# The sixth batch's routing in a fused block attention and top-1 expert kernel: begun a pair sooner, its small operations on GpSimd

## The chip, the cores and the metric

One core of one Trainium2 chip. The metric is device time of one execution in microseconds (us), the lower the better. Engines are named as the profile names them: PE is TensorE (PEld its weight loads), DVE is VectorE, ACT is ScalarE, POOL is GpSimd, SP is SyncE, which here only issues DMAs. The clock of TensorE has two levels, 1.2 and 2.4 GHz; the profile gives the granted share of the higher one.

## The reference

```python
# q, k, v: (8, 8, 576, 64)
mask = (pos[:, None] // 64) >= (pos[None, :] // 64)
attn = softmax(where(mask, q @ k.T / 8, -1e9))
x = (attn @ v) as 4608 tokens x 512
logits = x @ w_gate                     # 512 x 8
e_idx = argmax(logits, axis=1)
gate_w = softmax(logits)[row, e_idx]
eom = 1 / (1 + exp(-(x @ w_output_gate)))
for e in range(8):
    mask = e_idx == e
    out[mask] = gate_w[mask] * eom[mask, e] * (relu(x[mask] @ w1[e]) @ w2[e])
```

Block-causal attention over 8 batches of 8 heads; each of the 4608 tokens then goes to the one expert with its largest logit, and its result is scaled by two gates.

## The kernel before

**Attention.** Heads go in pairs, four pairs a batch, 32 pairs in all; one turn of the loop at L1208 attends one pair (`attend`, L1169). A turn interleaves three pairs: the scores and exponentials of pair p (`softmax`, L332), the transposes of pair p-1's probabilities (`flip`, L436) and the product with the values of pair p-2 (`values`, L472). The order on TensorE is written out by hand as a string in `attend`, of which each letter is one step: S scores, F a flip group, V values, t one tick.

```python
for x in "S.Ft.SVFSV.FttSFt.":
```

So a turn has four ticks, and every generator in the list `later` makes one step at each of them. Flip groups turn probabilities in the one PSUM tile `ps_f`, which ACT and DVE each copy half of into `pT` (L446); the next group waits until both have done so. The maxima of the scores (`nmx`, L375) are DVE's, the exponentials (L368, L419) ACT's. Q and K of a coming pair are split into two 16-bit parts by POOL (`split_qk`, L141, tiles `natq`, `natk`, `sp`) and turned by a DMA transpose that SP issues (`turn_qk`, L160, `qk<-sp`); there are three `qk` tiles, so the transpose of pair p+3 waits for the last scores of pair p (L413).

**Routing.** When a batch's values are done, a generator `finish_batch` (L504) is put into `later`. It makes the logits (L532), turns them (L571, L581), multiplies them by the reciprocal of the softmax sums, reduces over heads into `L` (L587), takes the maximum `mx`, and then runs a chain of small operations on tiles of 40 or 5 columns (`on_pool`, L595): `d`, `eq`, `er`, `oh` (the one-hot choice), `z`, then a prefix sum over tokens on TensorE (L672 to L678), the slot `sli`, and the gate by `se`, `zs` and a reciprocal into `idg` (L718). Five indirect DMAs on POOL, the scatters (L724), write token and gate into a table in DRAM, `tab_d`. `rows` (L508) turns the attention result by TensorE, scales it on DVE (`xn`, L516) and `store` (L524) sends it to `x_d` by SP.

The flag `slow` marks batches 0 to 4: their small operations go to POOL and are spread over ticks by `part`. Batches 5 to 7 keep them on DVE in one tick. For b == B - 3, the sixth batch (b = 5), the row blocks are moved out by a second generator, `spread_rows`. With a batch's values ending in the turn after its last pair but one, the sixth batch's route runs while pairs 26 to 29 are attended.

**Experts.** From pair 30 on, `route_first` (L761) picks the first expert from the counts of batches 0 to 5, `fetch_ids` (L908) reads the table after the scatters, `fetch_x` (L924) gathers tokens into `xg` and weights are loaded. The pool `ld`, which holds `natq`, `natk` and `sp`, is given back at L1215, and two of the `xg` tiles, which are cleared by POOL at L1222, lie in its place. Then steps of 256, 128 or 64 tokens pass through the experts (L1062, L1103) until the end, TensorE being busy almost throughout.

The order of a queue is not wholly the program's: within the marks `issue_after` and `behind`, a scheduler places instructions on ACT, DVE, POOL and SP. A queue is in order: what stands behind a waiting instruction waits too.

## Time and profile before

| | us |
|---|---|
| median of 3 runs | 738.97 |
| the three runs | 737.44, 738.97, 741.25 |
| the profiled execution | 742.68 |
| its span, first to last instruction | 741.1 |
| PE busy | 701.0 (95%) |
| DVE busy | 543.8 (73%) |
| ACT busy | 499.1 (67%) |
| POOL busy | 317.5 (43%) |

The profile tells one execution; its rows have the start in us from the span's start, the duration, the engine, the line, what is written and read, and in square brackets how long the engine stood idle before and what ended that ("issue" means that the profile shows no wait). An engine's share over the whole span says little here, as attention, hand-over and experts have different limits, so stretches are looked at one by one. The attention stage lies in about the first 325 us.

### The profile page before, as it was taken

Reading aid. Unit: us, or ns where it says so; the run is one execution under the profiler, and the core shown is the slowest. Engines: PE = TensorE matmul, PEld = TensorE weight load, DVE = VectorE, ACT = ScalarE, POOL = GpSimd, SP = SyncE. Lnnn points to the kernel's source line nnn. Section 1 sums busy time; section 2 is a strip of 40 time slices with the busy share of each in tenths; the row PEclk is TensorE's granted clock in tenths of the full one; section 3 lists DMA queues with packets and bytes.
Section 4 is the critical chain, followed back from the end, with each engine's and each line's share of the span. In section 5 each row is a group of like instructions: output and inputs, shape, how many; then the busy total and the mean of one; then the engine's idle time right before and its main releaser. Section 6 shows DMA issues by size and latency. Waiting matters only on the chain. (4 is left out here: it accounts for less than half of the span.)

```text
span 741.1 us, 21145 instructions
## 1 busy us (share of the span) xinstructions
PE 701.0 (95%) x8277; PEld 497.3 (67%) x8298; DVE 543.8 (73%) x948; ACT 499.1 (67%) x1097; POOL 317.5 (43%) x407
## 2 busy tenths in 40 slices
PE   5999999998999996989999999999999999999994
PEld 4677777766777764757568666876577676767761
DVE  4877988887888886887777658955588577858830
ACT  4888888886888875774356558765577487758630
POOL 4375468776686873015365523321223133311011
PEclk9999999999999998899999999999999999999998
DMA  7989898999999984458546796977999999775601
GB/s 199 215 189 208 142 206 146 168 195 187 201 211 184 177 129 74 131 171 233 138 143 130 215 283 191 296 91 241 259 302 363 247 335 321 273 224 195 237 31 46
DMA packets 235997, 146.85 MB, mean 198 GB/s; under 512 B 187120, under 2 KB 203568, under 8 KB 235888
## 3 DMA queue, kind: packets, MB, share of 16 engines
q1 hardware_dynamic: 227136, 125.85, 71.0%
q0 software_dynamic: 8208, 19.29, 9.1%
q8 instruction: 67, 1.10, 0.7%
q14 instruction: 42, 0.34, 0.2%
q10 hardware_dynamic: 544, 0.26, 0.1%
HBM read 126.43 MB, written 19.34 MB: 197 GB/s over the span
## 5 line engine op out<-in xcount | busy, mean ns | idle before, releaser
L1083 PEld LDWEIGHTS <-w1b 128*128 128x128 f16 (+1 forms) x2208 | 176.2, 98 | 25.9 <-issue 4.5
L1083 PE MATMUL ps_s<-xt,w1b 128*128 128x256 f16 (+5 forms) x1920 | 175.5, 253 | 0.7 <-DVE w1b L961 0.4
L1118 PE MATMUL ps_t<-w2b,hh 128*128 128x512 f16 (+1 forms) x539 | 162.1, 379 | 0.0
L961 DVE TENSOR_TENSOR w2b<-w2f,w2b 128x1024 bf16<-128x1024 f32 x80 | 92.9, 1222 | 83.3 <-ACT w2b L959 81.1
L375 DVE TENSOR_REDUCE nmx<-ps_s 128x1 f32<-128x512 f32 (+4 forms) x224 | 130.5, 617 | 24.4 <-PE ps_s L364 9.7
L368 ACT ACTIVATE pt<-ps_s,nmx 128x256 f32<-128x256 f32 (+3 forms) x256 | 132.6, 534 | 11.5 <-DVE nmx L375 6.8
L1126 POOL DMA_INDIRECT out_dram<-ys,ids x38 | 48.1, 1266 | 171.3 <-ACT ys L1125 93.6
L1118 PE MATMUL ps_t<-w2b,hl 128*128 128x512 f16 x280 | 106.1, 379 | 1.1
L961 DVE TENSOR_TENSOR w1b<-w1f,w1b 128x1024 bf16<-128x1024 f32 x80 | 93.5, 1220 | 8.9 <-ACT w1b L959 8.7
L1118 PEld LDWEIGHTS <-hh 128*128 128x128 f16 x560 | 54.4, 98 | 61.6
L1125 ACT ACTIVATE ys<-ps_t,ids 128x512 f32<-128x512 f32 (+1 forms) x38 | 25.9, 685 | 98.1 <-PE ps_t L1118 77.2
L959 ACT CAST w1b<-w1f 128x1024 f16<-128x1024 f32 x80 | 78.8, 1045 | 13.5 <-DMA w1f<-in_moe_w_dram 11.6
L482 PE MATMUL ps_t<-pT,vv 128*64 128x256 f32 (+3 forms) x512 | 83.7, 448 | 1.1 <-DVE sums L549 0.8
L446 DVE COPY pT<-ps_f 128x512 f32<-128x512 f32 x93 | 63.7, 685 | 25.2 <-PE ps_f L443 20.8
L356 PE MATMUL ps_s<-qk 64*128 64x256 f16 (+1 forms) x1152 | 72.2, 256 | 7.7 <-DMA qk<-sp 3.4
L959 ACT CAST w2b<-w2f 128x1024 f16<-128x1024 f32 x80 | 78.0, 1044 | 1.5 <-DMA w2f<-in_moe_w_dram 1.3
L928 POOL DMA_INDIRECT xg<-x_d,ids x38 | 54.3, 1428 | 31.5 <-issue 10.4
L356 PEld LDWEIGHTS <-qk 64*128 64x128 f16 x1152 | 47.3, 96 | 21.5 <-issue 13.8
L446 ACT COPY pT<-ps_f 128x512 f32<-128x512 f32 x93 | 54.6, 587 | 9.1 <-PE ps_f L443 5.3
L1091 ACT ACTIVATE hh<-ps_s 128x1024 f16<-128x1024 f32 (+2 forms) x46 | 38.9, 846 | 30.4 <-PE ps_s L1083 27.9
L443 PEld LDWEIGHTS ps_f<-ident,pt 64*128 64x128 f32 x1116 | 42.1, 138 | 25.3 <-ACT pt L368 11.4
L724 POOL DMA_INDIRECT tab_d<-idg,sli x40 | 41.9, 1048 | 38.3 <-DVE sli L692 30.5
(221 smaller groups left out, 1055.3 us busy)
## 6 DMA issues: line engine op xcount, KB each, us to landing
w1f<-in_moe_w_dram SPq DMA_DIRECT2D x80, 512.0 KB
w2f<-in_moe_w_dram SPq DMA_DIRECT2D x80, 512.0 KB
vv<-in_v_dram SPq DMA_DIRECT2D x64, 128.0 KB
x_d<-xn SPq DMA_DIRECT2D x32, 256.0 KB
natk<-in_k_dram SPq DMA_DIRECT2D x14, 512.0 KB
natq<-in_q_dram SPq DMA_DIRECT2D x28, 256.0 KB
hh<-in_moe_w_dram SPq DMA_DIRECT2D x4, 512.0 KB
hl<-in_moe_w_dram SPq DMA_DIRECT2D x4, 512.0 KB
```

The source lines that it names most:

```text
L356: nc.tensor.matmul(ps[:, ab, c:c + m], qk[rows, cq, P * t:P * t + P], cols(qk[rows, ck], x, kind), start=(i == 0), stop=(i == 2 and c + m ...
L368: last_exp[0] = nc.scalar.activation(probs[t][:, ab], ps[:, ab, c0:c0 + n], AF.Exp, bias=nmx[:, t, ab:ab + 1], accum_out=sums[:, t, 2 * hp ...
L375: last_max[0] = nc.vector.tensor_reduce(o, x, AX.X, ALU.max, negate=True)
L443: nc.tensor.transpose(ps[:, h, 64 * i:64 * i + 64], src[rows], ident[rows, rows])
L446: copy(to[:, h], ps[:, h].rearrange("p (s c) -> p s c", c=P))
L482: nc.tensor.matmul(pa[o, P * j:S0].rearrange("p (t h n) -> p t h n", h=2, n=64), vv[:, j, a0 + ab], pT[:, :, x:x + P * m].rearrange("p h ( ...
L928: nc.gpsimd.indirect_dma_start(out=xg[i % NXG][:, h], out_offset=None, in_=x_d[0:nx, :], in_offset=IOA(ap=ids[i][:, h, 0:1].bitcast(U32), ...
L959: nc.scalar.copy(hi, src)
L961: eng.tensor_tensor(lo, src, hi, ALU.subtract)
L1083: nc.tensor.matmul(ph[:, f4].rearrange("p (h n) -> p h n", n=w), wv[:, cc, f, :], xv[:, cc, :, 0:w], start=(k == 0), stop=(k == 3 * KD - 1))
L1118: nc.tensor.matmul(py, hv[:, f, h], wv[:, f, :], start=(k == 0), stop=(k == 3 * KF - 1))
L1126: nc.gpsimd.indirect_dma_start(out=out, out_offset=IOA(ap=ids[i][0:r, h, 0:1].bitcast(U32), axis=0), in_=ys[0:r], in_offset=None, bounds_c ...
```

## The change

It puts the sixth batch (flag `mid`) nearly onto the path of the batches ahead of it. Its wide logits come in the same tick as its narrow ones, and two ticks fall out, so that the maximum `mx` is taken in pair 26 in place of pair 27. `d`, `eq`, `oh`, the memset, `z`, `se` and `zs` go to POOL behind its last instruction; `er` and the choice come a few ticks later; `exp` of `d` comes earlier on ACT. `spread_rows` is gone, the row blocks are written out between the steps (last block in pair 27, blocks 0 and 1 in pair 28, 2 and 3 in pair 29). The scatters stand at the four ticks of pair 29.

```diff
@@ -539,7 +539,7 @@
         def keep(c0, c1, pm):
             nc.scalar.copy(lgT[:, c0:c1], pm[:, 0:c1 - c0])
 
-        held, rush = [], b == B - 1
+        held, rush, mid = [], b == B - 1, b == B - 3
         pm = ps_t.tile([P, 512], F32, name="ps_t")
         nc.tensor.matmul(pm[0:64, P:P + NP], ident[:, 64:128], sumL, start=True, stop=True)
         if not rush:
@@ -557,7 +557,8 @@
             yield
         else:
             keep(S0, S, pm)
-            yield
+            if not mid:
+                yield
             nc.scalar.activation(rec, sums, AF.Copy, bias=1e-9)
             pm = ps_t.tile([P, 512], F32, name="ps_t")
             logits(0, S0, pm)
@@ -565,7 +566,8 @@
             yield
             nc.vector.reciprocal(rec, rec)
             yield
-            yield
+            if not mid:
+                yield
         pm = ps_t.tile([P, 512], F32, name="ps_t")
         for t in range(LAST):
             nc.tensor.transpose(pm[:, P * t:P * t + P], lgT[:, Q0[t]:Q0[t] + P], ident)
@@ -590,36 +592,28 @@
         nc.vector.tensor_reduce(mx, lg, AX.X, ALU.max)
         mxb = mx.unsqueeze(2).broadcast_to([P, NT, E])
         slow = b < B - 3
-        eng = nc.gpsimd if slow else nc.vector
+        pool = slow or mid
+        eng = nc.gpsimd if pool else nc.vector
 
         def on_pool(*ops):
 
             for op, args in ops:
-                with behind() if slow else nullcontext():
+                with behind() if pool else nullcontext():
                     ins = getattr(eng, op)(*args)
-                if slow:
+                if pool:
                     last_pool[0] = ins
 
         def after(last):
-            return tc.issue_after(last[0].ins) if slow else nullcontext()
+            return tc.issue_after(last[0].ins) if pool else nullcontext()
 
         def part(n):
 
             for x in range(n if slow else 0):
                 yield
 
-        def part_rows(t):
-
-            if slow:
-                rows(t)
-                yield
-                store()
-
-        def spread_rows():
-
-            for n, t in ((2, LAST), (0, 0), (2, 1), (0, 2), (0, 3)):
-                for x in range(n):
-                    yield
+        def part_rows(t, always=False):
+
+            if slow or always:
                 rows(t)
                 yield
                 store()
@@ -630,16 +624,22 @@
         oh = small.tile([P, NT, E], F16, name="oh")
         z = small.tile([P, NT, E], F32, name="z")
         yield from part(3)
+        if mid:
+            yield
         on_pool(
             ("tensor_tensor", (d, lg, mxb, ALU.subtract)),
             ("tensor_scalar", (eq, d, 0.0, None, ALU.is_equal)),
             ("tensor_tensor", (eq, eq, erev.unsqueeze(1).broadcast_to([P, NT, E]), ALU.mult)),
         )
-        yield from part_rows(LAST)
+        if mid:
+            yield
+        yield from part_rows(LAST, mid)
         yield from part_rows(0)
         with after(last_max):
             nc.vector.tensor_reduce(er, eq, AX.X, ALU.max)
         yield from part(1)
+        if mid:
+            yield
         erb = er.unsqueeze(2).broadcast_to([P, NT, E])
         on_pool(
             ("tensor_tensor", (eq, erb, erev.unsqueeze(1).broadcast_to([P, NT, E]), ALU.subtract)),
@@ -647,18 +647,17 @@
             ("memset", (oh[64:128, LAST, :], 0.0)),
             ("tensor_tensor", (z, lz, oh, ALU.mult)),
         )
-        if slow:
+        if pool:
             with after(last_exp):
                 nc.scalar.activation(d, d, AF.Exp)
         yield from part(1)
         yield from part_rows(1)
         yield from part_rows(2)
         yield from part(1)
-        if b == B - 3:
-            later.append(spread_rows())
-            yield
-            yield
-            yield
+        if mid:
+            yield
+            yield from part_rows(0, True)
+            yield from part_rows(1, True)
             yield
         elif not slow:
             yield
@@ -690,7 +689,8 @@
         sli = small.tile([P, NT], I32, name="sli")
         if not slow:
             last_hot[0] = nc.vector.tensor_copy(sli, sl)
-            nc.scalar.activation(d, d, AF.Exp)
+            if not mid:
+                nc.scalar.activation(d, d, AF.Exp)
         se = small.tile([P, NT], F32, name="se")
         with after(last_max):
             nc.vector.tensor_reduce(se, d, AX.X, ALU.add)
@@ -699,6 +699,8 @@
             nc.vector.tensor_reduce(zs, z, AX.X, ALU.add)
         yield from part(1)
         yield from part_rows(3)
+        if mid:
+            yield
         with after(last_exp):
             last_gate[0] = nc.scalar.activation(zs, zs, AF.Exp, scale=-1.0)
         yield from part(1)
@@ -717,8 +719,14 @@
         with after(last_max):
             nc.vector.reciprocal(idg.bitcast(F32)[:, b, :, 1], zs)
         yield from part(2)
+        if mid:
+            rows(2)
         for t in range(NT):
             r = ROWS[t]
+            if mid and t in (1, 2):
+                store()
+            if mid and t == 1:
+                rows(3)
 
             with behind():
                 last_pool[0] = nc.gpsimd.indirect_dma_start(
@@ -733,8 +741,9 @@
             tc.add_to_no_dep_group("scatters", sc)
             scatters.append(sc)
             if b < B - 1 and t < LAST:
-                yield
-                if b < B - 3 or b == B - 3 and t == 0:
+                if not mid or t < 3:
+                    yield
+                if slow:
                     yield
         if rush:
             for t in range(NT):
```

Three places show what moved. On POOL, from the end of the split of pair 31 on, before (`se` and `zs` are the gate's tiles, `xg` the token tiles, `row` what `route_first` makes):

```order
L155 TENSOR_TENSOR sp<-natk_104,sp 128x2x4x64
L724 DMA tab_d<-idg,sli 37120x2 x6
L1222 MEMSET xg_6324 128x1024
L1222 MEMSET xg_6326 128x1024
L916 TENSOR_LOAD row_202
```

and now:

```order
L155 TENSOR_TENSOR sp<-natk_104,sp 128x2x4x64 [waits Pool_49]
L732 DMA tab_d<-idg,sli 37120x2 [waits DMASW5_49]
L602 TENSOR_SCALAR se<-se 128x5 [waits DVE_49]
L1231 MEMSET xg_6324 128x1024 [waits DMAHW3_49,DMAHW4_49,DMAHW0_49,Pool_49]
L1231 MEMSET xg_6326 128x1024
L602 TENSOR_SCALAR zs<-zs 128x5 [waits Activation_49]
L602 TENSOR_TENSOR zs<-zs,se 128x5 [waits Pool_49]
L732 DMA tab_d<-idg,sli 37120x2 [waits DMASW6_49,DVE_49]
L732 DMA tab_d<-idg,sli 37120x2 [waits DMASW7_49]
```

`se` and `zs` are new on this queue, and the two memsets, which wait for three DMA queues, stand ahead of `zs` and of the five scatters.

On DVE, pair 28, between its second maxima and its second copy of `pT`, before:

```order
L599 TENSOR_TENSOR eq<-er,erev 128x40 [waits DVE_49]
L696 TENSOR_REDUCE se<-d 128x5 [waits Activation_49]
L599 TENSOR_SCALAR oh<-eq 128x40 [waits DVE_49]
L599 TENSOR_SCALAR se<-se 128x5 [waits DVE_49]
L599 MEMSET oh 64x4 [waits DVE_49]
L599 TENSOR_TENSOR z<-L,oh 128x40 [waits DVE_49]
L683 TENSOR_REDUCE add<-oh 128x8
L699 TENSOR_REDUCE zs<-z 128x5 [waits DVE_49]
L685 TENSOR_TENSOR run_cnt<-run_cnt,add 128x8 [waits DVE_49]
L599 TENSOR_SCALAR zs<-zs 128x5 [waits Activation_49]
L599 TENSOR_TENSOR zs<-zs,se 128x5 [waits DVE_49]
L446 COPY pT<-ps_f 128x4x128 [waits PE_49]
```

and the same place now:

```order
L375 TENSOR_REDUCE nmx<-ps_s 128x1 [waits PE_49]
L375 TENSOR_REDUCE nmx<-ps_s 128x1
L446 COPY pT<-ps_f 128x4x128 [waits PE_49]
L394 TENSOR_REDUCE qlast_108<-qk 64x2x64 [waits DMAHW4_49]
L394 TENSOR_REDUCE qlast_108<-qk 64x2x64
L375 TENSOR_REDUCE nmx<-ps_s 128x1 [waits PE_49]
```

The chain between the maxima and the copy is gone. In pair 29 DVE now has, from the first copy of `pT` on:

```order
L446 COPY pT<-ps_f 128x4x128 [waits PE_49]
L516 TENSOR_TENSOR xn<-ps_t,rec 128x512 [waits DMAHW5_49,PE_49]
L375 TENSOR_REDUCE nmx<-ps_s 128x1 [waits PE_49]
L375 TENSOR_REDUCE nmx<-ps_s 128x1
L720 RECIPROCAL idg<-zs 128x5 [waits Pool_49]
L446 COPY pT<-ps_f 128x4x128 [waits PE_49]
L394 TENSOR_REDUCE qlast_109<-qk 64x2x64 [waits DMAHW3_49]
L394 TENSOR_REDUCE qlast_109<-qk 64x2x64
```

Here the sixth batch's reciprocal, which waits for POOL, stands between the second maxima (128x1) and the second copy of `pT`.

On PE, pair 26, behind its first flip group, before:

```order
L513 MATMUL ps_t<-ident,xT 128x128 [waits Activation_49]
L513 MATMUL ps_t<-ident,xT 128x128 x3
L544 MATMUL ps_t<-sumL,ident 64x4 [waits DVE_49]
L534 MATMUL ps_t<-xT,wg_bd 32x64 x4
L356 LDWEIGHTS qk
L356 MATMUL ps_s<-qk 128x256 [waits Activation_49]
```

and now:

```order
L513 MATMUL ps_t<-ident,xT 128x128 [waits Activation_49]
L513 MATMUL ps_t<-ident,xT 128x128 x3
L544 MATMUL ps_t<-sumL,ident 64x4 [waits DVE_49]
L534 MATMUL ps_t<-xT,wg_bd 32x64 x4
L534 MATMUL ps_t<-xT,wg_bd 32x512 [waits DVE_49]
L534 MATMUL ps_t<-xT,wg_bd 32x512 x3
L356 LDWEIGHTS qk
L356 MATMUL ps_s<-qk 128x256 [waits Activation_49]
```

The wide logits (32x512) stand ahead of the next scores and wait for DVE.

## Rows read from the trace of the kernel before

**Rows 1.** Stretches of pairs 25 to 29: us, busy us by engine, PEclk, DMA share, GB/s

```profile
243.30:252.20 8.90, 8.90 (x149) 6.74 (x147) 7.73 (x16) 7.49 (x24) 8.12 (x14) 1.00 1.20 203
252.20:262.70 10.50, 10.34 (x170) 7.02 (x168) 8.06 (x23) 8.39 (x27) 5.48 (x12) 1.00 0.68 166
262.70:271.60 8.90, 8.90 (x152) 6.52 (x152) 7.55 (x17) 7.29 (x23) 8.29 (x12) 1.00 0.82 128
271.60:286.00 14.40, 10.54 (x153) 7.72 (x148) 12.81 (x35) 8.29 (x27) 6.25 (x7) 0.91 0.53 62
286.00:301.40 15.40, 13.10 (x153) 9.60 (x152) 9.21 (x18) 7.59 (x23) 6.64 (x7) 0.75 0.46 75
```

**Rows 2.** Order of time on PE, pairs 28 and 29

```profile
281.51 0.46 PE L443 MATMUL ps_f<-ident,pt 64*128 64x64 f32 x8 [2.69 <-DVE pT L446]
...
283.41 1.11 PE L513 MATMUL ps_t<-ident,xT 128*128 128x128 f32 x4 [0.92 <-DVE xT L499]
284.32 1.65 PE L413 MATMUL ps_s<-qk,qlast 128*128 128x256 f16 x9
...
293.11 0.41 PE L356 MATMUL ps_s<-qk 64*128 64x256 f16 x4 [0.96 <-issue]
294.54 0.58 PE L356 MATMUL ps_s<-qk 64*128 64x256 f16 x3 [1.02 <-issue]
```

**Rows 3.** Order of time on PE, pairs 26 and 27

```profile
261.71 0.92 PE L413 MATMUL ps_s<-qk,qlast 128*128 128x256 f16 x9
...
269.57 0.46 PE L443 MATMUL ps_f<-ident,pt 64*128 64x64 f32 x8
```

**Rows 4.** Order of time on DVE, pair 28

```profile
275.54 1.83 DVE L599 TENSOR_SCALAR eq<-d 128x40 f32<-128x40 f32 x1
...
280.60 0.17 DVE L599 TENSOR_TENSOR zs<-zs,se 128x5 f32<-128x5 f32 x1
280.68 0.68 DVE L446 COPY pT<-ps_f 128x512 f32<-128x512 f32 x1
```

**Rows 5.** Instructions of L599: ns shortest/median/longest, first and last start, form

```profile
L599 POOL TENSOR_SCALAR eq<-d x5: 331/332/332, 84.6 to 237.7; 128x40 f32<-128x40 f32 x5
...
L599 POOL TENSOR_SCALAR zs<-zs x5: 231/232/234, 109.2 to 262.2; 128x5 f32<-128x5 f32 x5
...
L599 DVE TENSOR_SCALAR eq<-d x3: 185/195/1828, 275.5 to 345.8; 128x40 f32<-128x40 f32 x3
```

**Rows 6.** Order of time on POOL, pairs 24 to 30

```profile
237.36 0.25 POOL L599 TENSOR_TENSOR d<-L,mx 128x40 f32<-128x40 f32 x1 [3.50 <-DVE mx L590]
...
276.17 1.16 POOL L155 TENSOR_TENSOR sp<-natk,sp 128x512 f16<-128x512 f32 x1
...
287.35 0.99 POOL L724 DMA_INDIRECT tab_d<-idg,sli  x1 [8.95 <-DVE sli L692]
...
293.79 1.84 POOL L1222 MEMSET xg<- 128x1024 f32 x2 [0.42 <-issue]
308.42 0.78 POOL L917 DMA_DIRECT2D ids<-tab_d  x1 [12.78 <-DVE qlast L394]
```

**Rows 7.** Order of time on DVE, pairs 26 and 27

```profile
254.97 0.68 DVE L516 TENSOR_TENSOR xn<-ps_t,rec 128x512 f32<-128x512 f32 x1
...
267.62 0.69 DVE L446 COPY pT<-ps_f 128x512 f32<-128x512 f32 x1 [0.70 <-PE ps_f L443]
```

**Rows 8.** Order of time on PE, pair 26, the narrow logits

```profile
254.60 0.32 PE L534 MATMUL ps_t<-xT,wg_bd 128*32 128x64 f32 x8
```

**Rows 9.** Order of time on SP, two transposes of Q and K

```profile
167.16 6.07 SPq L164 DMA_TRANSPOSE qk<-sp  x1
...
286.04 2.72 SPq L164 DMA_TRANSPOSE qk<-sp  x1
```

**Rows 10.** Order of time on PE, scores that waited for the first of these

```profile
177.98 0.34 PE L356 MATMUL ps_s<-qk 64*128 64x128 f16 x6 [1.60 <-DMA qk<-sp]
```

**Rows 11.** DMA share in tenths, 284 to 294 us in 40 equal slices

```profile
DMA  0000000000000899998069999799899992501321
```

## The prediction

> **What bounds the kernel now.** I number pairs 0 to 31 and write p28 for pair 28; the sixth batch is b = 5, its values end in p25, its route runs in p26 to p29. I first cut the attention stage into pairs, from one last row maximum (L375 of 576 columns) to the next [rows 1]. p25 to p27 take 8.90, 10.50 and 8.90 us, 9.43 on average, with TensorE busy in all but 0.16 us: here TensorE sets the pace, and GpSimd's and DVE's small work is free while it hides beside it. Then p28 takes 14.40 and p29 15.40, 5.0 and 6.0 us over that average, at granted clocks of 0.91 and 0.75. These two pairs are the only place where the change can win much.
>
> Next I asked why TensorE stands there, in its order of time [rows 2]. In p28 it stops for 2.69 us until 281.51, released by DVE's copy of pT (the copy frees the PSUM tile ps_f for the next flip group), then for 0.92 us until 283.41; right after it nine L413 matmuls take 1.65 us where p26's took 0.92 [rows 3], with the granted clock down between its two levels, 1.2 and 2.4 GHz (0.91 over the pair). In p29 it stops for 0.96 and 1.02 us inside one group of score matmuls, released by "issue": no wait that the profile shows.
>
> Then DVE's order [rows 4]: the copy that TensorE waited for started at 280.68, late because the route's chain stands ahead of it on the same engine, among it one eq of 1.83 us. The same instruction takes 0.185 us when nothing disturbs it [rows 5]. It ran while GpSimd's subtraction of 276.17 to 277.33 ran [rows 6]. In p26 the end of L413 was at 262.63 (261.71 + 0.92) [rows 3], and the like copy started at 267.62 [rows 7], 4.99 after it. This is the measure used below: T is the end of a pair's L413, and the next pair's second copy of pT starts at T + 5.0 when nothing is late. The third flip group, which needs it, starts at 269.57 [rows 3], T + 6.9; so the copy has a slack of 6.9 - 5.0 - 0.69 = 1.2 us.
>
> **The change part by part.**
> *The chain leaves DVE.* d, eq twice, the second eq, oh, se, the memset, z and the zs pair go to GpSimd, ten instructions, and exp of d no longer stands between two pairs of exponentials on ScalarE. GpSimd pays 0.23 to 0.33 us for such an operation [rows 5], beside DVE's and TensorE's work. With the chain gone, p28 has nothing that other pairs lack: -5.0.
>
> Here a page and the rows can be weighed. The eq of 1.83 us overlaps GpSimd's subtraction, as said. The Trainium skill, "SBUF — State Buffer", section "Who interferes with whom", says that VectorE and GpSimd share one port pair under an exclusive lock that is held for a whole instruction. By that rule 1.64 of eq is a wait that ends when eq itself stands in GpSimd's queue, and the -5.0 stands; were it a cost of that place in DVE's order, another instruction would inherit it and the sum would be 1.64 higher. No row separates the two.
>
> *A pair sooner.* The 512 column logits now stand right behind the 64 column ones in p26, and take the ps_t buffer whose xn DVE finishes at 255.65 (254.97 + 0.68) [rows 7]; TensorE is ready for them at 254.92 (254.60 + 0.32) [rows 8]. +0.7. The transposes of lgT and the reduction L move from p27 and p28 to p26; the 1.24 us of L now delay p27's first maxima instead of p28's. Unhidden they are +1.24, fully hidden 0; with DVE busy in 7.55 of p27's 8.90 us [rows 1] I take +0.4. Together +1.1.
>
> *GpSimd's queue.* d waits for mx: in the fourth batch such a wait took 3.50 us [rows 6]. The split of p31 ended at 277.33 before [rows 6]; waits, three operations and two scatters ahead of it make it some 4 us later, about 281. It is needed when the transpose of p31 may start, which is the end of p28's L413 (284.32 + 1.65 = 285.97 [rows 2], SP issues at 286.04 [rows 9]); in the changed kernel that end comes at about 281.7. It just fits: 0. The er reduction comes three steps after its inputs: 0.
>
> *The stores.* The 64 row store goes ahead of vlast and one 256 KB store ahead of p31's transpose on SP. Each is ready some 5 us earlier, and one store less runs beside the transpose: 0.
>
> *The new wait.* This is the term that decides. GpSimd's order is now: se, two memsets of xg, the two zs operations, the scatters. The memsets wait for the transposes of p29, p30 and p31, because xg lies where their sources lay. And DVE's reciprocal of zs stands right ahead of p29's second copy of pT and waits for the zs operations. Before, the memsets stood behind the scatters and nobody waited for them [rows 6]. So p29's copy now waits for the landing of p31's transpose. Let L be the time from its issue, at about T + 0.1, to its landing. Behind it come two memsets (1.84 us [rows 6]), twice some 0.23 for zs [rows 5], and some 0.5 for the reciprocal and the handovers, an estimate from the 0.17 of a like small operation on DVE [rows 4]: the copy starts at about T + L + 2.8, and the third flip group at T + L + 3.5. The stall is L + 3.5 - 6.9 = L - 3.4. Bounds of L: at least the 2.72 us that SP takes to issue it [rows 9]; at most 10.8, as the one issued at 167.16 [rows 9] released TensorE at 177.98 [rows 10]. For p31's own, the DMA share stays high until about 292.5 [rows 11] (slices of 0.25 us from 284), 6.5 us after its issue. I take 6.5, the same transfer: +3.1. At the ends it is 0 and +7.4.
>
> *The scatters.* They now start behind the reciprocal, at some T + 9, five that took 6.0 us from 287.35 to the idle 0.42 us ahead of the memset [rows 6], and end near T + 15. The first read of the table is issued at 308.42, after 12.78 us of idle [rows 6]; that cover shrinks to some 3 us. I price it at 0; if the landing needs more than those 3 us, the first gathers are late.
>
> *The gaps of p29.* Its 6.0 us are gaps without a visible wait and the half clock behind them. They begin while GpSimd issues five scatters in a row from 287.35 on [rows 6], and p29 had just come out of a slow stretch; both conditions leave that place. Bounds: all stay, 0; all go, -6.0.
>
> **The sum** against the profiled execution (742.68, span 741.1 and 1.6 around it): -5.0 + 1.1 + 3.1 = -0.8. With the gaps kept 741.9, with the gaps gone 735.9. The median of the runs, 738.97, lies 3.7 below the profiled one, so the typical run seems to hold only part of those gaps: from it, -0.8 gives 738.2. I expect between 735.9 and 738.2, nearer the lower end: **736.6**.
>
> **The rivals.**
> *The new wait costs nothing, the gaps go* (faster). If L is below 3.4 the stall vanishes; for it speaks that fewer transfers run beside p31's transpose, against it the 6.5 us of the same transfer. Time: 742.68 - 5.0 + 1.1 - 6.0 = 732.8.
> *The transpose lands late* (slower). With L = 10.8 the stall is 7.4, and TensorE may fall to half clock behind it as at 283.41, which I price at the 0.73 us by which those L413 grew [rows 2, 3] and about as much again for the rest, 1.4. From the median: 738.97 - 5.0 + 1.1 + 7.4 + 1.4 = 743.9. It is slower than before from L = 7.3 on (L - 3.4 over 3.9). For it: p31's transpose and the wait are now in one chain with no slack. Against it: the 10.8 was in a stretch with V, Q and K loads in the queues.
> *It moves nothing*: p28's loss merely walks to p29 with its clock: 738.97.
> *GpSimd is too slow for the chain.* Its eq takes 0.332 where DVE's shortest is 0.185 [rows 5]; ten such add 1 to 1.5 us. If it is late with eq in p27, er holds DVE's queue: +1.5, 740.5 from the median. [...]
>
> **How the numbers follow.** Forecast (735.3 to 739): 0.50. Free wait with gaps gone: 0.27. Late landing: 0.12. Nothing: 0.07. Slow GpSimd: 0.04. About 0.5%, 3.7 us, is what a measurement here can tell from no change; that is under 735.3 and over 742.7. The forecast gives 0.06 of its own to faster, the free wait all of its 0.27; the late landing gives 0.10 to slower, the rest is in between: 0.33, 0.57, 0.10. The range reaches from just under the free-wait case to a stall with L near 9: **732.0 to 741.5**.
>
> **What would show it.** p28 near 9.5 us, with no stall on DVE's pT copy and eq on GpSimd at 0.33; p26 with a wait of some 0.7 us ahead of the logits. In p29 GpSimd's first memset released by the DMA of qk, DVE idle before the reciprocal until GpSimd's zs, TensorE idle some 3 us ahead of its third flip group. I am wrong if the reciprocal does not wait, if p28 stays above 12 us, or if TensorE's stall in p29 is over 5 us.

## The result, and the profile after

The changed kernel took 743.47 us in the median of 21 runs (738.4 to 750.47), the kernel before 738.76 in 21 runs beside them: ratio 1.0078, 95% interval 1.0054 to 1.0102. Slower by 0.8%, and 2.0 us above the range's upper end. A ratio, here and below, leaves out executions more than 1.5% above the fastest of their kernel, so it can differ from the quotient of the medians beside it. The change's profiled execution took 744.06, span 742.1.

First the same cut into pairs as in [rows 1], here for p26 to p30 of the changed kernel (us, busy us by engine, PEclk, DMA share, GB/s; the last line sums them):

```profile
258.64:270.22 11.58, 10.79 (x174) 7.45 (x172) 8.82 (x24) 8.61 (x27) 1.26 (x4) 1.00 0.77 198
270.22:279.41 9.19, 8.89 (x146) 6.54 (x144) 8.78 (x20) 7.52 (x23) 6.59 (x12) 1.00 0.76 124
279.41:288.40 8.99, 8.99 (x149) 6.72 (x147) 7.79 (x16) 7.53 (x25) 8.20 (x14) 1.00 0.80 91
288.40:302.96 14.56, 10.81 (x156) 8.04 (x154) 8.54 (x24) 7.72 (x24) 7.43 (x11) 0.88 0.45 101
302.96:312.70 9.74, 9.55 (x160) 6.43 (x158) 8.19 (x28) 8.28 (x26) 3.16 (x4) 1.00 0.33 83
sum 54.06, PE 49.03 PEld 35.18 DVE 42.11 ACT 39.67 POOL 26.64; mean PE 9.81 PEld 7.04 DVE 8.42 ACT 7.93 POOL 5.33
```

p28 fell from 14.40 to 8.99 with TensorE busy throughout: its loss is gone. p26 grew by 1.08, p27 by 0.29. p29 still takes 14.56, but for another reason. TensorE, order of time, in p26 and p29:

```profile
262.15 1.07 PE L534 MATMUL ps_t<-xT,wg_bd 128*32 128x512 f32 x8 [0.79 <-DVE sums L549]
...
299.39 0.69 PE L443 MATMUL ps_f<-ident,pt 64*128 64x64 f32 x8 [3.75 <-DVE pT L446]
...
301.35 1.57 PE L413 MATMUL ps_s<-qk,qlast 128*128 128x256 f16 x9
```

The wide logits wait 0.79 us; in p29 the third flip group waits 3.75 us for DVE's copy, and TensorE runs at half clock behind it (granted clock 0.53 from 299.4 to 302.9; L413 takes 1.57 where [rows 3] has 0.92). DVE, order of time, in the same place:

```profile
292.00 1.01 DVE L375 TENSOR_REDUCE nmx<-ps_s 128x1 f32<-128x384 f32 x2
298.49 0.19 DVE L720 RECIPROCAL idg<-zs 128x5 f32<-128x5 f32 x1 [5.47 <-POOL zs L602]
298.59 0.65 DVE L446 COPY pT<-ps_f 128x512 f32<-128x512 f32 x1
```

DVE stood for 5.47 us before the reciprocal, for GpSimd's zs. GpSimd, order of time:

```profile
288.10 1.16 POOL L155 TENSOR_TENSOR sp<-natk,sp 128x512 f16<-128x512 f32 x1
...
290.49 0.25 POOL L602 TENSOR_SCALAR se<-se 128x5 f32<-128x5 f32 x1
296.13 1.84 POOL L1231 MEMSET xg<- 128x1024 f32 x2 [5.40 <-DMA qk<-sp]
297.94 0.23 POOL L602 TENSOR_SCALAR zs<-zs 128x5 f32<-128x5 f32 x1
298.26 0.20 POOL L602 TENSOR_TENSOR zs<-zs,se 128x5 f32<-128x5 f32 x1
298.96 1.08 POOL L732 DMA_INDIRECT tab_d<-idg,sli  x1 [0.51 <-DVE idg L720]
```

and SP's issue of p31's transpose:

```profile
289.28 3.45 SPq L164 DMA_TRANSPOSE qk<-sp  x1
```

So the chain is the one predicted: transpose issued at 289.28, landed when the memset starts (296.13, 6.85 later), two memsets, zs, reciprocal, copy, flip group. In p26 to p30 the change nevertheless took less than the profiled execution of before, 54.06 against 59.00 (the last four stretches of [rows 1] and p30's 9.80). The whole profiled execution is 1.4 us longer all the same, because the changed kernel's met two late transposes ahead of p26 (p17 and p25, 17.2 and 13.2 us against 10.8 and 9.0), where both kernels have the same instructions in the same order. In p17 TensorE waited for one of them:

```profile
169.30 0.50 PE L356 MATMUL ps_s<-qk 64*128 64x128 f16 x6 [6.53 <-DMA qk<-sp]
```

One execution of each could therefore not tell what the change cost.

### The profile page after: what moved, and what is told of

The parts are those of the page before. It is cut to its first block, busy times and chain, and to the rows that moved or that the text cites. A ratio compares the mean times of both kernels' runs of the same rounds, so it can differ in the third digit from the quotient of the medians.

```text
span 742.1 us, 21165 instructions
## 1 busy us (share of the span) xinstructions
PE 699.9 (94%) x8298; PEld 495.8 (67%) x8298; DVE 540.8 (73%) x938; ACT 499.2 (67%) x1097; POOL 315.6 (43%) x417
## 3 DMA queue, kind: packets, MB, share of 16 engines
q1 hardware_dynamic: 227136, 125.85, 70.6%
## 5 line engine op out<-in xcount | busy, mean ns | idle before, releaser
L1127 PE MATMUL ps_t<-w2b,hh 128*128 128x512 f16 (+1 forms) x560 | 166.6, 379 | 0.0
L375 DVE TENSOR_REDUCE nmx<-ps_s 128x1 f32<-128x512 f32 (+4 forms) x224 | 130.4, 618 | 25.1 <-PE ps_s L364 16.6
L368 ACT ACTIVATE pt<-ps_s,nmx 128x256 f32<-128x256 f32 (+3 forms) x256 | 132.6, 533 | 11.9 <-DVE nmx L375 11.2
L1135 POOL DMA_INDIRECT out_dram<-ys,ids x38 | 46.4, 1220 | 175.4 <-ACT ys L1134 88.6
L356 PE MATMUL ps_s<-qk 64*128 64x256 f16 (+1 forms) x1152 | 71.9, 256 | 11.8 <-DMA qk<-sp 9.8
L937 POOL DMA_INDIRECT xg<-x_d,ids x38 | 52.2, 1375 | 28.3 <-issue 7.7
L356 PEld LDWEIGHTS <-qk 64*128 64x128 f16 x1152 | 46.5, 96 | 25.9 <-issue 10.8
L443 PE MATMUL ps_f<-ident,pt 64*128 64x64 f32 x1116 | 54.8, 233 | 4.9 <-DVE pT L446 3.7
```

The costliest lines, as they stand in the source:

```text
L356: nc.tensor.matmul(ps[:, ab, c:c + m], qk[rows, cq, P * t:P * t + P], cols(qk[rows, ck], x, kind), start=(i == 0), stop=(i == 2 and c + m ...
L368: last_exp[0] = nc.scalar.activation(probs[t][:, ab], ps[:, ab, c0:c0 + n], AF.Exp, bias=nmx[:, t, ab:ab + 1], accum_out=sums[:, t, 2 * hp ...
L375: last_max[0] = nc.vector.tensor_reduce(o, x, AX.X, ALU.max, negate=True)
L443: nc.tensor.transpose(ps[:, h, 64 * i:64 * i + 64], src[rows], ident[rows, rows])
L937: nc.gpsimd.indirect_dma_start(out=xg[i % NXG][:, h], out_offset=None, in_=x_d[0:nx, :], in_offset=IOA(ap=ids[i][:, h, 0:1].bitcast(U32), ...
L1127: nc.tensor.matmul(py, hv[:, f, h], wv[:, f, :], start=(k == 0), stop=(k == 3 * KF - 1))
```

## The experiments

The runs come in groups; each group shared one chip and the runs of the kernel before on it. Where I give periods of pairs they run from the start of one pair's L413 to the next one's, read from the order of time on TensorE. The profiled executions of r2_before and r4_memset_last were long for their kernels (756.45 and 740.31 us, medians 750.76 and 737.74); they are left out of the readings except where I name them, and their medians stand.

**Both kernels once more; the memsets last; the chain on DVE.** r1_before and r1_after are copies.

> The kernel before once more, unchanged, for a second trace and for what chance does. Theory W (the wait): the change costs time because p29's reciprocal stands behind the two memsets of xg and these behind p31's transpose, and the profiled execution of before was a bad one: its p28 and p29, 14.0 and 16.1 us from one L413 to the next, take some 4 to 9 us less together in a usual execution; so p26 to p31 near 61 to 65 us here where the first trace had 69.6. Theory E (elsewhere): p28 and p29 lose their 11 us in every execution (p26 to p31 again 68 to 71), and the change gains there but pays more at places whose code it does not touch (p17, p25) or among the experts. Timed against itself: ratio 1.000, the interval a few tenths of a per cent wide.

> The changed kernel once more, for a second trace. Theory W: p29 again 13 to 15 us with DVE idle for 5 to 6 us before the reciprocal; p17 and p25, 17.2 and 13.2 us in the first trace, fall back to 9 to 11 or the loss turns up in other pairs, since those were late transposes that any execution can meet. Theory E: p17 and p25 lose 6 and 4 us again.

e1_memset_last:

```diff
-                nc.gpsimd.memset(xg[j], 0.0)
+                with behind():
+                    last_pool[0] = nc.gpsimd.memset(xg[j], 0.0)
```

> The change with the two memsets of xg kept behind the sixth batch's scatters on GpSimd, as they stood before. Theory W: DVE's reciprocal no longer waits, p29 takes 9 to 10 us in place of 13.9, and the kernel is 4 to 5 us faster than the change: about 739, the same as before within 0.5%. Theory E: p29 gains its 4.9 us in the trace, but the time stays over 741, since the loss lies elsewhere.

e2_chain_on_dve, in `finish_batch` of the changed kernel:

```diff
-        eng = nc.gpsimd if pool else nc.vector
+        eng = nc.gpsimd if slow else nc.vector
...
-                with behind() if pool else nullcontext():
+                with behind() if slow else nullcontext():
...
-                if pool:
+                if slow:
                     last_pool[0] = ins
```

> The change with the sixth batch's small operations (d, eq, oh, z, se, zs) back on DVE, but begun a pair sooner and spread over the ticks as the change has them; the memsets stay ahead of the scatters. Theory W: zs and the reciprocal no longer hang on GpSimd, so p29 takes 9 to 10 us and the time is as in the run with the memsets last, about 739 (the memsets still wait some 5 us for the transpose, and nobody waits for them). A rival within W: an eq on DVE takes 1.8 us beside GpSimd's splits as in the kernel before, holds a copy of pT, and 1 to 4 us come back in p27 or p28: 740 to 743. Theory E: over 741 whatever p27 to p29 do.

Measured: before against itself 740.85 and 740.98 (ratio 0.9937, 0.9883 to 0.9991: the interval of one group can miss 1 by a little). The change in a single execution 745.91. Memsets last 737.19, 3.8 under before: 0.9944 (0.9909 to 0.9980). Chain on DVE 738.99: 0.9967 (0.9931 to 1.0004). Second stretches of the kernel before, p28 and p29, and the sum over p26 to p30:

```profile
274.71:288.37 13.66, 10.30 (x155) 7.58 (x154) 12.36 (x36) 8.28 (x27) 6.48 (x7) 0.93 0.62 66
288.37:299.40 11.03, 10.12 (x151) 7.43 (x150) 8.08 (x17) 7.69 (x23) 6.65 (x7) 0.93 0.70 104
...
sum 53.93, PE 49.11 PEld 35.03 DVE 44.87 ACT 39.49 POOL 23.62; mean PE 9.82 PEld 7.01 DVE 8.97 ACT 7.90 POOL 4.72
```

p28's loss is there again, p29's gaps are not: 53.93 in all, as much as the change's 54.06. Theory W had asked for that. The second trace of the change has p29 at 13.98 (13.90 first, by L413), p17 at 13.1, p25 at 13.7; p25 takes 13.7 in r1_before too, so that loss is not the change's. In the run with the memsets last:

```profile
288.03:297.29 9.26, 9.26 (x156) 6.96 (x154) 8.68 (x24) 7.61 (x24) 5.53 (x8) 1.00 0.69 160
...
sum 49.51, PE 47.54 PEld 34.14 DVE 42.33 ACT 39.49 POOL 30.39; mean PE 9.51 PEld 6.83 DVE 8.47 ACT 7.90 POOL 6.08
```

p29 is 9.26 and the wait is gone; DVE there, and then GpSimd:

```profile
293.00 0.19 DVE L720 RECIPROCAL idg<-zs 128x5 f32<-128x5 f32 x1 [0.35 <-POOL zs L602]
293.26 0.69 DVE L446 COPY pT<-ps_f 128x512 f32<-128x512 f32 x1
```

```profile
292.46 0.23 POOL L602 TENSOR_SCALAR zs<-zs 128x5 f32<-128x5 f32 x1 [2.10 <-ACT zs L705]
...
299.55 1.87 POOL L1232 MEMSET xg<- 128x1024 f32 x2
```

With the chain on DVE the memset waits even longer, and nobody minds (p29 9.24); p28 keeps two stalls. GpSimd, then TensorE:

```profile
293.08 1.84 POOL L1231 MEMSET xg<- 128x1024 f32 x2 [9.33 <-DMA qk<-sp]
```

```profile
278.33 0.71 PE L443 MATMUL ps_f<-ident,pt 64*128 64x64 f32 x16 [0.68 <-DVE pT L446]
...
280.36 0.67 PE L356 MATMUL ps_s<-qk 64*128 64x256 f16 x12 [0.73 <-ACT plast L419]
```

So it is not the memsets' wait that costs, but that the reciprocal hangs on it.

**The change timed again; the wide logits apart; GpSimd without the earlier start.** r2_before and r2_after are copies, on a chip where everything took some 10 us more.

> A third trace of the kernel before. The first two gave 69.6 and 63.0 us for p26 to p31, p28 at 14.0 and 12.9 and p29 at 16.1 and 10.9. If p28's loss belongs to the kernel and p29's to one execution only, p28 is again 12.5 to 14, p29 10 to 11.5, and p26 to p31 62 to 64. If p29's gaps are usual, p29 is over 14 again.

> The changed kernel timed once more on the same chip as the others, with a third trace. Theory W2 (one wait for another): p28's 4 to 5 us are won and p29's 4.9 are paid in every execution, p26 to p31 63.1 to 63.5 as in the two traces so far, so it stands at 0.997 to 1.005 of before, and the 0.8% measured first is partly the luck of late transposes ahead of p26, where both kernels have the same order of instructions. Theory S (slower by itself): it is again 0.5 to 1.0% slower than before although p26 to p31 takes the same 63 us, and the loss shows ahead of p26 or among the experts.

e3_wide_logits_apart, against e1_memset_last:

```diff
             keep(S0, S, pm)
-            if not mid:
-                yield
+            yield
...
-        if not rush:
+        if not rush and not mid:
             yield
         pm = ps_t.tile([P, 512], F32, name="ps_t")
         nc.tensor.transpose(pm[0:64, 0:P], lgT[:, S0:S], ident)
```

> The run with the memsets last, and beside that the wide logits one step behind the narrow ones again (the small transposition of the logits moves into the step of the large ones, so that the maximum stays where the change has it). Expected: p26 falls from 11.6 to about 10.5, since TensorE no longer waits 0.8 us for the PSUM tile; p27 to p31 stay within 0.3 us each (p27 9.2, p29 9.3); 57.5 for p26 to p31 in place of 58.6, 0.8 to 1.2 us faster than the run with the memsets last: about 736, 4 to 5 under before. Rival: the large logits now stand ahead of L413 in p26, and the transposition of the logits waits for ScalarE's copy of them: then 0.5 to 1.5 us come back as a gap of TensorE ahead of p27's first scores.

e4_gpsimd_not_sooner, against the kernel before:

```diff
-        eng = nc.gpsimd if slow else nc.vector
+        mid = b == B - 3
+        pool = slow or mid
+        eng = nc.gpsimd if pool else nc.vector
...
```

with `pool` for `slow` in `on_pool`, `after` and at the early exp of `d`, and the late one left out for this batch.

> The kernel before with the sixth batch's small operations on GpSimd and nothing else of the change: begun as late as before, scatters and row blocks as before (the memsets fall behind the scatters). If the place on DVE beside GpSimd's splits is what costs p28 its 4 to 5 us, p28 falls to 9 to 10.5. But er now waits for GpSimd in the middle of p28 (d, eq, eq take some 1 us there), and the reciprocal for zs behind the split of p31, both on DVE with maxima behind them: p28 or p29 keeps 1 to 3 us; p26 to p31 60 to 62, and the time 0.997 of before. If the earlier start is needed for the gain, p28 and p29 together stay over 22 as in before.

Measured: before 750.66 (r2_before 750.76); the change 752.98, 1.0053 (1.0014 to 1.0092), p29 14.0. Logits apart 747.73, 2.9 under before, though the ratio shows nothing clear (0.9997, 0.9962 to 1.0033). p26 did fall to 10.45, and p27 rose from 9.20 to 9.91, where DVE's reciprocal of the fifth batch (b = 4) now releases the flip group:

```profile
276.56 0.58 PE L443 MATMUL ps_f<-ident,pt 64*128 64x64 f32 x12 [0.39 <-DVE idg L719]
```

So 0.4 us net, not 1.1. GpSimd alone took 749.86: 1.0035 (0.9994 to 1.0076), no gain that can be told. p28 11.2, p29 14.7, in which TensorE waits 1.45 us for a copy and stands in gaps without a visible wait. Of the two halves the earlier start alone (e2, on another chip) did better against before, 0.9967; neither ratio is clear of 1.

**The change and the run with the memsets last on one chip.** Copies of the change, of e1 and of e2.

> The changed kernel a third time, on one chip with the next two. It has stood at 1.008 and 1.005 of before. If p29's wait is all of its loss against the run with the memsets last, it stands 4 to 6 us over that run here, and 0 to 5 over before; p29 again 13.9 to 14.1 us, p31's transpose landing 6.7 to 6.9 us after its issue.

> The change with the memsets last once more, beside the changed kernel on the same chip: 4 to 6 us faster than it (p29 at 9.3 in place of 14.0), and 2 to 5 us faster than before. If the wait were not the cause, the two would stand within 1.5 us.

> The earlier start with the small operations on DVE once more on the same chip: what the move to GpSimd is worth by itself. In the first pair of traces p28 took 10.6 us here and 9.0 with the operations on GpSimd, so 0.5 to 2 us slower than the run with the memsets last, and still 1 to 4 us faster than before.

Measured: before 743.30; change 744.77, 1.0022 (0.9985 to 1.0060); memsets last 740.11, 0.9995 (0.9956 to 1.0034); chain on DVE 742.32, 0.9995. The change stands 4.7 us over the run with the memsets last, as theory W asked, in the medians (3.1 in the means, with 95% within 2.6 of it); p29 13.3 against 9.26. p30 is long in all three traces: 12.8 us in the change, mostly half clock behind p29's wait (granted clock 0.84), but 16.2 and 16.4 in the others for TensorE's gaps and the half clock behind them (0.79). So the traces of the change and of the memsets last, 55.9 and 55.2 us for p26 to p30, do not show the 4.7 on this chip; those of the first group, 54.3 and 49.5, do. GpSimd and TensorE in r3_memset_last:

```profile
288.55 1.08 POOL L732 DMA_INDIRECT tab_d<-idg,sli  x1 [0.50 <-DVE idg L720]
...
293.75 0.91 POOL L732 DMA_INDIRECT tab_d<-idg,sli  x1 [0.31 <-issue]
```

```profile
292.47 0.44 PE L468 MATMUL ps_t<-ident,pt 128*128 128x128 f32 x2 [0.62 <-issue]
293.65 0.19 PE L364 MATMUL ps_s<-mneg,mrow 64*128 64x64 bf16 x1 [0.45 <-issue]
294.36 0.19 PE L364 MATMUL ps_s<-mneg,mrow 64*128 64x64 bf16 x1 [0.53 <-issue]
295.78 0.58 PE L356 MATMUL ps_s<-qk 64*128 64x256 f16 x3 [1.02 <-issue]
```

Five scatters start 1.27 to 1.39 us apart from 288.55 on; the first gap ends 3.9 us later. In [rows 2, 6] it was much the same: scatters from 287.35, gaps before 293.11 and 294.54, and a first one of 0.32 before 291.7. The change has its scatters in a row too (298.96 to 304, the last four 0.30 us after one another), for they all wait behind the reciprocal: standing at four steps in the program spread nothing.

**The scatters apart.** r4_memset_last is e1 again. e6_scatters_apart is e1 with pauses between the sixth batch's scatters; they multiply a tile that nothing reads:

```diff
+    pause = const.tile([P, 40], F32, name="pause")
+    nc.gpsimd.memset(pause, 0.0)
...
             sc = last_pool[0].ins
+            for x in range(4 if b == B - 3 and t < LAST else 0):
+                with behind():
+                    last_pool[0] = nc.gpsimd.tensor_tensor(pause, pause, pause, ALU.mult)
```

e9_apart_and_logits has e3's edit beside it; e10_change_apart puts the pauses into the change itself.

> The change with the memsets last, the measure for the next three on this chip. In the two traces so far p26 to p31 took 58.6 and 65.4 us; the 6.4 us of difference are p30 (9.7 and 16.2), where TensorE stood in gaps without a visible wait from 3.9 us after the first of five scatters in a row on GpSimd, and half clock behind them. If that is the scatters' doing, it is 9.7 or 16 here again, by the chip.

> The run with the memsets last, and four small multiplications of a dead 40 column tile on GpSimd behind each scatter but the last, so that the scatters start some 1.6 to 2.7 us apart instead of 1.27. If scatters in a row cause TensorE's gaps (theory G), p30 takes 9.7 to 11 us in any execution, and on a chip where the run with the memsets last has its gaps this one is 3 to 6 us faster; the first read of the table starts some 2 to 4 us later and its cover takes that. If the gaps come from something else at that time (theory O: code loading, the landing of the weights), p30 is again near 16 where the other run has it so, and the times agree within 1.5 us.

> The scatters apart, the memsets last, and the wide logits a step behind the narrow ones: p26 10.5, p27 9.9, p28 9.0, p29 9.3, p30 10 to 11 by theory G: 0.3 to 0.6 us faster than the run with the scatters apart, and 4 to 9 us faster than before. By theory O within 1 us of the run with the memsets last.

> The change as it is, with the scatters apart and nothing else. p29 keeps its wait, 13.3 to 14 us. Theory G: p30 falls to 9.8 to 10.5 where the changed kernel had 10.4 to 12.8: 0 to 2.5 us faster than the change, so 1 to 4 us slower than the run with the scatters apart and the memsets last. The table's reads start later, since the scatters now end near 309: if the cover behind them is gone, the first gathers and the experts' start come 1 to 3 us late, and it is as slow as the change or slower.

Measured: before 741.76; memsets last 737.74, 0.9936 (0.9896 to 0.9977); scatters apart 744.04, 1.0018; with the logits 742.81, 1.0026; change apart 747.72, 1.0081 (1.0045 to 1.0118). Neither theory's time held: e6 is 6.3 us slower than the run with the memsets last, where G wanted it faster or equal and O equal. p30 was free of gaps with pauses (9.74 in e6, 10.15 in e9, 11.12 in e10 behind p29's wait of 13.2), but no trace without them on this chip shows gaps to be rid of; the only one is of 0.37 in e9's p29, ahead of its sixth batch's scatters. The 6.3 us showed as no stall in e6's trace, whose execution was the shortest of its twelve (738.04).

**The pauses or the place.** The tile of 160 bytes had moved nearly every other tile of the attention stage by 160 bytes, and many of the experts' with them. r5_memset_last is e1 again; e11_apart_512 is e6 with `pause` of 128 columns, 512 bytes, and the pauses on its first 40; e12_shift_only is e1 with the 160 byte tile and its memset, no pauses.

> The change with the memsets last a fourth time, the measure for the next two on this chip: 0.993 to 1.000 of before.

> The scatters apart as in the earlier run, but the tile that the pauses work on takes 512 bytes of a partition and not 160. The 160 had moved almost every other tile of the kernel by 160 bytes, so that tiles which began at multiples of 512 (natq, natk, vlast) no longer did; all three runs with it were slower than before (1.0018, 1.0026, 1.0081). Theory A (place): with 512 bytes the starts are multiples of 512 again, the loss of 5 to 6 us against the run with the memsets last goes, and the pauses' own worth shows: 0 where that run has no gaps in p30, 3 to 6 us faster where it has. Theory P (pauses): it stays 4 to 7 us slower than the run with the memsets last, since the table is read later.

> The change with the memsets last, and the 160 byte tile put in and cleared once, with no pauses: nothing is changed but where other tiles lie. Theory A: 4 to 7 us slower than the run with the memsets last. Theory P: the same as that run within 1.5 us.

Measured: before 746.31; memsets last 740.16, 0.9950 (0.9916 to 0.9984); 512 bytes 742.42, 0.9962 (0.9929 to 0.9994); the shift alone 746.24, 1.0012 (0.9975 to 1.0048): 6.1 us for moving tiles, theory A (4.9 in the means, with 95% within 2.8 of it). The pauses themselves bring nothing here (2.3 us over memsets last in the median, 0.9 in the means, with 95% within 2.5). The page's DMA queue row of r5_memset_last, of e12_shift_only and of e11_apart_512 (packets, MB, share of 16 engines):

```profile
q1 hardware_dynamic: 227136, 125.85, 71.7%
```

```profile
q1 hardware_dynamic: 227136, 125.85, 74.5%
```

```profile
q1 hardware_dynamic: 227136, 125.85, 71.6%
```

The same packets take more of the DMA engines' time when the tiles are moved by 160 bytes. Every trace without the shift lies between 70.1 and 71.9%, the four with it (e6, e9, e10, e12) between 74.5 and 76.3%. It is the packets of 256 bytes, 177,152 of that queue's 227,136, that grew: 24.6 to 26.3 ns each on average in the traces without the shift, 27.2 to 28.3 in the four with it; those of 512, 2048 and 4096 bytes do not separate the two.

## Why the prediction was wrong, point by point

The forecast was 6.9 us under the result. Of these, 1.6 are gaps that it credited to the change, 0.9 the terms of its sum, and some 4.4 stay open, as told below.

**The chain leaves DVE, -5.0: right in p28, and it took more with it.** By the pair stretches p28 went from 14.40 and 13.66 to 8.99. Another 2.2 us of p29 and p30 go too where the new wait is away: 11.03 and 10.17 in the second trace of before, 9.26 and 9.74 in the run with the memsets last. What the forecast quotes of the Trainium skill, "SBUF — State Buffer", section "Who interferes with whom", fits the second trace of before: there another instruction took 1.69 us and ended with GpSimd's subtraction, while eq took its short time; DVE, then GpSimd:

```profile
278.36 0.17 DVE L599 TENSOR_SCALAR eq<-d 128x40 f32<-128x40 f32 x1
...
279.05 1.69 DVE L599 TENSOR_TENSOR eq<-eq,erev 128x40 f32<-128x40 f32 x1
```

```profile
279.51 1.17 POOL L155 TENSOR_TENSOR sp<-natk,sp 128x512 f16<-128x512 f32 x1
```

It ends (280.74) when the subtraction does (280.68), so the cost belongs to the overlap and not to one instruction; in the changed kernel p28 has nothing that inherits it. Both slow instructions started while a scatter of GpSimd's ran ahead of the subtraction (278.48 to 279.48 here), so what held them in their first 0.5 us is not shown. With the chain on DVE, but begun sooner and spread (e2), p28 loses 1.7 us (10.64 against 8.98 by L413).

**A pair sooner, +1.1: somewhat small.** p26 +1.13 and p27 +0.57 against the second trace of before, 1.7; 0.79 of it is the wait on the tile, which was given as 0.7.

**GpSimd's queue, "It just fits: 0": wrong by 0.9 us.** p31's split ended at 289.26, L413 of p28 at 288.36 (287.45 + 0.91), and SP issued the transpose at 289.28, T + 0.9 instead of T + 0.1.

**The new wait, +3.1: the mechanism right, the term too small.** The landing took 6.85 us where 6.5 was taken; in the three other traces of the change 7.03, 6.98 and 6.28 (from SP's issue to the memset's start). The stall was 3.75, 3.91, 3.91 and 3.19. In the first trace another 1.6 us of half clock came behind it (0.7 in L413, 1.57 for 0.91, and 0.9 in the flips and the transposition), which had no place in the forecast, only in a rival. Against the run with the memsets last p29 and p30 together cost 5.3 us by L413 (24.30 against 18.99). So the three terms measure -6.9, +1.7 and +5.3, where the forecast had -5.0, +1.1 and +3.1; that the two large errors nearly cancel is luck.

**The scatters, 0: right.** They end later, and nothing behind them is late for it: from p31's L413 to the end it is 418.6 to 421.8 us in the four traces of the change and 420.2 to 420.9 in the three of before (r2_before with them).

**The gaps of p29, 1.6 us of them counted as a gain: the step that failed.** The sum -0.8 was made against a profiled execution 3.7 above the median. From the median it gives 738.2, which leaves 2.3 us of gaps (6.0 - 3.7) in a typical execution; the 736.6 credits the change with taking away 1.6 of them. But the gaps are no property of the kernel before. They go by the chip: all three readable traces of the second group show them (1.1 us and more of gaps in p28 to p30), in the third two clearly and the change with one of 0.19, none of the four of the first group and none of the three of the last. Where they came, the change and the run with the memsets last had them too, behind their own scatters. A pair far ahead of them tells the two kinds of execution apart: p12 takes 9.55 to 9.74 us in every trace of the second and third groups, and 8.95 to 9.01 in those of the others. In the first trace of before it takes 9.59, in the first of the change 8.95; p12 from L413 to L413 on TensorE, before, then after:

```profile
117.24 0.91 PE L413 MATMUL ps_s<-qk,qlast 128*128 128x256 f16 x9
...
126.84 0.91 PE L413 MATMUL ps_s<-qk,qlast 128*128 128x256 f16 x9
```

```profile
115.65 0.91 PE L413 MATMUL ps_s<-qk,qlast 128*128 128x256 f16 x9
...
124.60 0.91 PE L413 MATMUL ps_s<-qk,qlast 128*128 128x256 f16 x9
```

So the forecast priced a loss of one kind of execution, and the profile after is of the other.

With the terms as measured in executions without gaps (p26 to p30, 53.93 to 54.06) the change is worth +0.1, so the forecast should have stood near 739. With gaps the change is even the shorter one there (by L413 58.94 in the first trace of before; 56.54 and 55.86 in the change, on other chips). The measured medians are 4.7, 2.3 and 1.5 us above before. The third group's interval (from 0.9985) still holds +0.1; the second's (from 1.0014) and the first measurement's (from 1.0054) do not. What lies beyond +0.1 is **open**. By the traces it would have to stand ahead of p26, where both kernels have identical instructions and tile places. L413 of p25 stands at 257.7, 258.8, 260.9 and 256.2 in the four traces of the change, at 251.3 and 254.7 in two of before (262.8 in r2_before), and at 251.9 to 256.6 in three of the run with the memsets last (260.9 in r4_memset_last), which is the change's program up to there. These are late transposes; p17 alone takes between 9.7 and 21.3 us. Whether they come later with the change or by chance, four traces can't tell, and so it stays unknown whether a step of the forecast is behind these 4.4 us.

**The rivals.** *The transpose lands late* named 743.9, within 0.4 us of the result, with L = 10.8; L was 6.9. The number was right by luck. *Free wait, gaps gone* fell with L over 3.4. *It moves nothing* is closest to the traces, though for a loss exchanged and not walked on. *GpSimd too slow* did not happen: p28 takes 8.98 us with the chain on GpSimd and 10.64 and 10.65 with it on DVE, and by the medians of two groups GpSimd is 1.8 and 2.2 us faster (737.19 and 740.11 against 738.99 and 742.32), though neither of these is clear of noise. The Trainium skill, "GPSIMD Engine Reference", section "4.1 Engine selection", would leave such work on VectorE, with GpSimd about 2 times slower for two-input operations and one-input ones at roughly line rate. At 128x40 the first trace of before shows something else: the two-input eq<-eq,erev takes 1.3 times as long on GpSimd (0.27 us against 0.20), the one-input eq<-d 1.7 times (0.33 against 0.20; medians). The operations are slower there, but stand where nobody waits.

**A version that beats both:** the change with the memsets kept behind the scatters, 3.8, 3.2, 4.0 and 6.2 us under before by the medians of four groups, and 49.51 against 53.93 us in p26 to p30. In three of the four its interval lies under 1; in the third group its ratio is 0.9995, so nothing is shown there.

## What to carry to other kernels

Work that is moved to a quiet queue inherits every wait of that queue: list what will stand ahead of it, and pin a wait that nobody needs (a clear for later use) behind the work that others wait for; two lines gave back 4.7 us here, by the medians of the one chip on which both were timed twelve times. A loss that one profiled execution shows and that no instruction of the program explains is to be seen in a second trace before a change is credited with removing it; and if the sum starts from the median, that loss is already partly out. A test kernel that adds a tile must keep the places of the other tiles, or carry a control that moves them alone.

## What the runs showed of the hardware

Moving the tiles by 160 bytes, so that those of the attention stage that transfers fill no longer start at multiples of 512 bytes of a partition, made the kernel 6.1 us slower in the median (746.24 against 740.16), and the same 227,136 DMA packets took 74.5% instead of 71.7% of the engines' span: the 256-byte ones 27.2 ns each instead of 25.1. Pairs that waited for nothing grew by 0.01 to 0.02 us each (8.63 to 8.65). Moved by 512 bytes they cost none of that (71.6%, 25.5 ns). As 160 is no multiple of 64, 128 or 256 either, which boundary counts isn't shown.

TensorE's gaps without a visible wait were seen or not seen by chip: 16.2 us for p30 on one, 9.7 in both traces on another, same kernel. In the traces that have them the first one of p29 or p30 ends 3.6 to 7.2 us behind the first of a row of scatters on GpSimd, some 1.3 us apart; smaller ones (up to 0.41) stand in p31, over 15 us behind the last scatter. Whether the spacing causes them stays open, since on the chips on which the pauses ran no row of the sixth batch's scatters has gaps behind it.
